# Output projection weights in two loads, powers of two one pass earlier, six mixer products ahead

## The chip, the cores and the metric

One core of one Trainium2 chip runs the kernel. The metric is the device time of one execution in microseconds (us); the figure for a kernel is the median of several runs. Engines are called by the names of the profile: PE multiplies matrices (PEld is its loading of the stationary operand), DVE and ACT work on vectors, POOL is hardly used here, SP issues most of the DMA transfers and ACT a few.

## The reference, cut to what matters

```
g = sigmoid((x * gate_w).sum(-1))                 # one gate per row
qkv = x @ wqkv                                    # 32 heads of 32
o = softmax(q . k at 8 positions, 2 apart) @ v    # sliding dilated window
a = o @ wo
z = gelu(x @ w_in); z1, z2 = z[:, :1792], layernorm(z[:, 1792:])
b = (z1 * (w_sp @ z2 + b_sp[:, None])) @ w_out    # mixer
out = g * a + (1 - g) * b                         # 2048 x 1024, bf16
```

## The kernel before, in words

All large buffers are regions of one tile in on-chip memory, `arena`, addressed by offsets. PSUM, the accumulation memory, is used as eight banks of 128x512; each product takes a bank and gives it back when the vector engines have read it.

PE works through these stages in order: the second half of z, the q/k/v projection (L478), the rest of z (L259, L515), the spatial mixing by w_sp in chunks of 512 output rows (`g_chunk`, L529), and then the output rows in sixteen blocks of 128, four blocks to a `final_chunk`. Rows 0 to 1023 of the mixing are plain products in `g_chunk(0)` and `g_chunk(1)`; rows 1024 to 2047 are done by `seven_products` (L645), seven half-size products in place of eight, between `final_chunk(1)` and `final_chunk(2)`. For these, the rows of w_sp are scaled by powers of two: `natural` loads 128 rows from ACT's queue (L570), `row_sums` (ACT) or `row_sums_fast` (DVE, L577) sums their absolute values, `row_powers` (DVE, L587 to L593) makes the powers, `scale_rows` multiplies on ACT (L611) and writes the rows to `wsp_d` from ACT's queue (L612), and `load_wsp` (L426) reads them back transposed on SP's queue.

The attention runs on DVE beside PE. For each of eight head groups `attention_steps` has a pass of q times k for two halves (L303 and the folds L306), the softmax, and a pass of probabilities times v for two halves (the product L336, the folds L342 and L343, the last one L339). The passes are software pipelined: group 7's q.k comes ahead of group 6's product with v, and group 7's product with v is last. q, k and v of a group are loaded to `q_t`, `k_t` and `v_t`, next to each other at `A_OFF`; the results of two groups are stored to `o_d` by `store_o` (L354).

One output block is, for each half of 512 columns, an attention product of 8 matmuls (`attn_mm`, L542, which needs the block of `o_d` transposed by `load_oT`, L397, in one of three slots, and `wo`), a mixer product of 14 matmuls (`mixer_mm`, L558), and `combine`: ACT scales the attention product (L565), DVE adds the mixer product (L566). Then SP stores the block (L739). `final_chunk(0)` makes the mixer products of blocks 0 and 1 (four of them, each holding a bank) ahead of everything else, and then calls `scaled_rows`.

wo lies at `A_OFF` as eight k tiles of 1024 columns, in the place of q, k and v and the beginning of the work buffer. `load_wo` makes four transfers (L394), one for each head of a group: head h goes to every fourth partition.

The order is written out by hand: a clock, `beat`, runs along with PE's columns; `beat.at(t, fn)` issues a piece of work when the clock passes t; DVE's steps carry their own lengths. That fixes each engine's order of instructions and each queue's order of transfers; only waits decide the times. Transfers signal eight counters in turn, and a transfer waits for the last one that had its counter. SP's queue at the end of the attention holds, in order: the load of v for group 7 (L350), the last `store_o`, the four of `load_wo`, `load_oT` for blocks 0, 1 and 2, `load_wsp(3, 0..3)`, the store of block 0, `load_oT(3)`, the store of block 1, `load_oT(4)`.

Of the kernel before, what the change touches and what calls it, by code (L numbers as in the profile page):

```python
# [17 lines left out]
D = 1024  # L18
KT = D // P
NH = 32  # L20
DH = 32
HG = 4
# [33 lines left out]
def kernel(  # L56
# [24 lines left out]
    def reg(off, n):  # L81
        return arena[:, off:off + n]
# [21 lines left out]
    for jh in range(2):  # L104
        for w in range(W):
            n = min(8, max(0, 14 - 2 * w - 8 * jh))
# [38 lines left out]
    wo_sb = reg(A_OFF, KT * D).rearrange("p (k n) -> p k n", k=KT)  # L145
# [38 lines left out]
    wo_v = A_wo.rearrange("(g h d) n -> g h d n", g=NG, h=HG, d=DH)  # L184
    sync = nc.sync
# [38 lines left out]
    beat = Beat()  # L224
# [74 lines left out]
    def qk_steps(jh):  # L299
        def mul():  # L300
            in0 = _sub_ap(q_t, (8 * jh) * C, [[0, W], [C, 8], [1, C]])
            in1 = _sub_ap(k_t, (8 * jh) * C, [[2 * C, W], [C, 8], [1, C]])
            TT(prod.rearrange("p (w j c) -> p w j c", w=W, j=8, c=C), in0, in1, ALU.mult)  # L303

        def fold(half):
            return lambda: TT(pv[:, :, 0:half], pv[:, :, 0:half], pv[:, :, half:2 * half], ALU.add)  # L306

        def last():
            TT(L[:, jh * 256:(jh + 1) * 256], pv[:, :, 0], pv[:, :, 1], ALU.add)

        return [(4.4, mul), (2.3, fold(16)), (1.2, fold(8)), (0.7, fold(4)), (0.6, fold(2)), (0.6, last)]
# [18 lines left out]
    def pv_steps(g, jh):  # L330
        o_out = obuf[:, :, (g % 2) * C:(g % 2 + 1) * C]

        def mul():
            in0 = _sub_ap(v_t, (8 * jh) * C, [[2 * C, W], [C, 8], [HG, DH], [1, HG]])
            in1 = _sub_ap(att_A, jh * 256, [[32, W], [HG, 8], [0, DH], [1, HG]])
            TT(prod.rearrange("p (w j d h) -> p w j d h", w=W, j=8, d=DH, h=HG), in0, in1, ALU.mult)  # L336

        def last():
            TT(o_out[:, 8 * jh:8 * jh + 8, :], p3[:, 0, :].rearrange("p (j c) -> p j c", c=C),  # L339
               p3[:, 1, :].rearrange("p (j c) -> p j c", c=C), ALU.add)  # L340

        return [(4.4, mul), (2.3, lambda: TT(p3[:, 0:4, :], p3[:, 0:4, :], p3[:, 4:8, :], ALU.add)),  # L342
                (1.2, lambda: TT(p3[:, 0:2, :], p3[:, 0:2, :], p3[:, 2:4, :], ALU.add)), (0.7, last)]  # L343

    def load_qk(g):
        sync.dma_start(q_t, bass.AP(tensor=q_d.tensor, offset=q_d.offset + g * S * C, ap=[[NJ * C, P], [1, NJ * C]]))
        sync.dma_start(k_t, bass.AP(tensor=k_d.tensor, offset=k_d.offset + (g * (S + 16) + 2) * C, ap=[[NJ * C, P], [1, NJJ * C]]))

    def load_v(g):
        sync.dma_start(v_t, bass.AP(tensor=v_d.tensor, offset=v_d.offset + (g * (S + 16) + 2) * C, ap=[[NJ * C, P], [1, NJJ * C]]))  # L350

    def store_o(g):
        dst = o_d[:, (g - 1) * C:(g + 1) * C].rearrange("(p j) c -> p j c", j=NJ)
        sync.dma_start(dst, obuf)  # L354

    def attention_steps(t):
        beat.at(t - 8.0, lambda: load_qk(0))
        beat.at(t - 7.9, lambda: load_v(0))
        for g in range(NG):
            for took, fn in qk_steps(0) + qk_steps(1):  # L360
                yield t, took, fn
            t = beat.vector
            if g + 1 < NG:
                beat.at(t + 1.0, lambda g=g: load_qk(g + 1))
            yield t, 2.4, soft_a
            t = beat.vector
            beat.at(t + (1.0 if g == 0 else 5.0), soft_exp)
            if g == 0:
                t += 5.0
            else:  # L370
                for took, fn in pv_steps(g - 1, 0) + pv_steps(g - 1, 1):
                    yield t, took, fn
                t = beat.vector
                if g + 1 < NG:
                    beat.at(t + 1.0, lambda g=g: load_v(g))
                else:
                    load_v(g)
                if g % 2 == 0:
                    beat.at(t + 1.5, lambda g=g: store_o(g - 1))
            yield t, 2.3, soft_b  # L380
            t = beat.vector
        for took, fn in pv_steps(NG - 1, 0) + pv_steps(NG - 1, 1):
            yield t + 5.0, took, fn
        t = beat.vector
        beat.at(t + 1.0, lambda: store_o(NG - 1))
        beat.at(t + 1.5, load_wo)
        for a in range(3):
            beat.at(t + 8.0, lambda a=a: load_oT(a))

    def load_wo():  # L390
        pitch = wo_sb.ap[0][0]
        for h in range(HG):
            dst = bass.AP(tensor=wo_sb.tensor, offset=wo_sb.offset + h * pitch, ap=[[pitch * HG, DH], [D, KT], [1, D]])
            sync.dma_start(dst, wo_v[:, h, :, :].rearrange("g d n -> d g n"))  # L394

    def load_oT(a):
        sync.dma_start_transpose(oT_slots[a % 3], o_d[a * P:(a + 1) * P, :])  # L397
# [141 lines left out]
    def attn_mm(a, n0, nw):  # L539
        psa = psum.tile([P, 512], F32, name="psa", tag="ps")  # L540
        for kt in range(KT):
            nc.tensor.matmul(psa[:, 0:nw], oT_slots[a % 3][:, kt, :], wo_sb[:, kt, n0:n0 + nw],  # L542
                             start=(kt == 0), stop=(kt == KT - 1))
        beat.run(KT * nw)
        return psa
# [9 lines left out]
    def mixer_mm(a, n0, nw):  # L555
        psb = psum.tile([P, 512], F32, name="psb", tag="ps")
        for f in range(NF):
            nc.tensor.matmul(psb[:, 0:nw], u_tile(f, a), w_out_sb[:, f, n0:n0 + nw],  # L558
                             start=(f == 0), stop=(f == NF - 1))
        beat.run(NF * nw)  # L560
        return psb
# [10 lines left out]
    def row_sums(r):  # L572
        for k in range(4):
            nc.scalar.activation(abs_out, nat_slots[r][:, 512 * k:512 * (k + 1)], ACT.Abs, accum_out=l1[:, r, k:k + 1])
# [9 lines left out]
    def row_powers(r0, r1, parts):  # L584
        v = nc.vector
        sl = slice(r0, r1)
        v.tensor_reduce(row[:, sl], l1[:, sl, 0:parts], AX.X, ALU.add)  # L587
        v.scalar_tensor_tensor(row[:, sl], b_in[:, sl], -1.0, row[:, sl], ALU.mult, ALU.max)
        TT(row[:, sl], row[:, sl], b_in[:, sl], ALU.max)
        v.tensor_scalar(row[:, sl], row[:, sl], TINY, None, ALU.max)  # L590
        v.tensor_scalar(expo[:, sl], row[:, sl].bitcast(I32), 23, None, ALU.logical_shift_right)
        v.tensor_scalar(up[:, sl], expo[:, sl], -1, 254 + TOP, ALU.mult, ALU.add)
        v.tensor_scalar(up[:, sl], up[:, sl], 23, None, ALU.logical_shift_left)  # L593
        beat.on_vector(0.9)
# [15 lines left out]
    def scale_rows(r):  # L610
        nc.scalar.activation(nat_slots[r], nat_slots[r], ACT.Copy, scale=up[:, r:r + 1].bitcast(F32))  # L611
        nc.scalar.dma_start(wsp_d[r], nat_slots[r])  # L612
# [101 lines left out]
    def final_chunk(c):  # L714
        first = {}
        if c == 0:
            for a in range(2):
                for n0 in (0, 512):
                    first[a, n0] = mixer_mm(a, n0, 512)
            beat.flush(1e9)  # L720
            scaled_rows()
        if c == 1:
            for k in range(5):
                beat.at(beat.now + 12.0 + 3.0 * k, lambda k=k: t_sums(k))
            for k in range(2):
                beat.at(beat.now + 28.0 + k, lambda k=k: s_sum(0, k))
        for a in range(4 * c, 4 * c + 4):
            ob = ob_slots[a % 3]
            if a > 0 and a + 2 < 16:
                load_oT(a + 2)  # L730
            last = a == 15
            for part, (n0, nw) in enumerate(((0, 512), (512, 384), (896, 128)) if last else ((0, 512), (512, 512))):
                psa = attn_mm(a, n0, nw)
                psb = first[a, n0] if (a, n0) in first else mixer_mm(a, n0, nw)
                combine(a, n0, nw, part % 2, psa, psb)
                if last:
                    sync.dma_start(out2[a * P:(a + 1) * P, n0:n0 + nw], ob[:, n0:n0 + nw])
            if not last:
                sync.dma_start(out2[a * P:(a + 1) * P, :], ob)  # L739
# [8 lines left out]
    t_rows = beat.now  # L748
    for k, r in enumerate((3, 4, 5, 6, 7)):
        natural(r)  # L750
        beat.at(t_rows + 6.0 + 3.5 * k, lambda r=r: row_sums(r))
        beat.at(t_rows + 32.0 + 3.0 * k, lambda r=r: scale_rows(r))
    beat.at(t_rows + 27.0, lambda: row_powers(3, 8, 4))
    beat.at(t_rows + 40.0, lambda: natural(0))
    g_chunk(1)
    final_chunk(0)
# [38 lines left out]
```

## Time and profile before

| | us |
|---|---|
| median of 3 runs | 710.26 (709.88 to 710.59) |
| the profiled execution | 711.12 |
| its span, first to last instruction | 709.3 |
| PE busy | 699.6 |
| DVE busy | 458.5 |
| ACT busy | 278.7 |

The span is 1.8 us shorter than the execution that it was taken from, and that execution is 0.9 us above the median. Start times in the profile are us from the start of the span; PE's granted clock is 0.998 on average over the span.

### The profile page before, as it was taken

To read this page: it belongs to the slowest core of one execution; us is meant where nothing else is said; L and a number is where in the kernel's file an instruction comes from. 1 tells how busy PE (TensorE), PEld (TensorE's weight loads), DVE (VectorE), ACT (ScalarE), POOL (GpSimd) and SP (SyncE) were. 2 spreads that over 40 slices of the span, in tenths; PEclk is the share of its full clock that TensorE was granted. 3 is DMA by queue.
4 is the path that set the end of the run, shared out by engine and by line. 5 is a ranking of instruction groups with operands and counts; after the bars stand their busy time and mean duration, and the time that the engine had idled before them with its cause. 6 is when DMAs were issued, how large, how long until landed. Compare 5 with 4: busy or idle time off the path is not lost. (4 is left out here: it accounts for less than half of the span.)

```text
span 709.3 us, 8465 instructions
## 1 busy us (share of the span) xinstructions
PE 699.6 (99%) x3319; PEld 359.6 (51%) x3319; DVE 458.5 (65%) x496; ACT 278.7 (39%) x508; POOL 14.0 (2%) x23
## 2 busy tenths in 40 slices
PE   8999999999999999999999999989999999999998
PEld 4466666666665554444444444434444444444444
DVE  0000498999999999999999999734153565731111
ACT  4434544435369886244341229435111222221111
POOL 1000000000000211000000000000000000000000
PEclk9999999999999999999999999999999999999999
DMA  9984974885573133885349940299942211202210
GB/s 227 192 178 97 259 192 113 216 192 157 145 203 121 56 101 60 210 287 175 107 142 276 357 169 36 76 351 261 179 112 67 69 33 57 45 0 60 60 44 31
DMA packets 182903, 101.29 MB, mean 143 GB/s; under 512 B 145744, under 2 KB 171344, under 8 KB 182608
## 3 DMA queue, kind: packets, MB, share of 16 engines
q1 hardware_dynamic: 180560, 92.37, 49.3%
q10 hardware_dynamic: 2304, 8.39, 3.2%
q8 instruction: 26, 0.43, 0.3%
q14 instruction: 13, 0.11, 0.0%
HBM read 51.91 MB, written 32.57 MB: 119 GB/s over the span
## 5 line engine op out<-in xcount | busy, mean ns | idle before, releaser
L478 PE MATMUL ps<-arena 128*128 128x512 bf16 x768 | 165.9, 379 | 0.0
L478 PEld LDWEIGHTS <-arena 128*128 128x128 bf16 x768 | 110.7, 144 | 55.1
L303 DVE TENSOR_TENSOR arena<-arena 128x8192 bf16<-128x8192 bf16 x16 | 70.8, 4423 | 53.2 <-DMA arena<-k_d 53.0
L558 PE MATMUL psb<-arena 128*128 128x512 bf16 (+2 forms) x462 | 101.6, 373 | 0.0
L259 PE MATMUL ps<-arena 128*128 128x512 bf16 (+1 forms) x512 | 97.7, 353 | 1.5 <-DMA arena<-in_B_w_in_dram 1.5
L529 PE MATMUL ps<-arena 128*128 128x512 bf16 x448 | 97.0, 379 | 0.0
L515 PE MATMUL ps<-arena 128*128 128x512 bf16 x448 | 96.9, 379 | 0.0
L481 ACT CAST arena<-ps 128x512 bf16<-128x512 f32 x96 | 55.8, 587 | 93.1 <-PE ps L478 88.6
L566 DVE SCALAR_TENSOR_TENSOR arena<-psb,omg,arena 128x512 bf16<-128x512 f32 (+2 forms) x33 | 24.2, 735 | 103.7 <-PE psb L558 88.3
L645 PE MATMUL ps<-arena 128*128 128x512 bf16 (+1 forms) x392 | 84.8, 379 | 0.0
L306 DVE TENSOR_TENSOR arena<-arena 128x4096 bf16<-128x4096 bf16 (+1 forms) x64 | 77.5, 1211 | 1.9
L259 PEld LDWEIGHTS <-arena 128*128 128x128 bf16 x512 | 50.0, 98 | 48.7 <-issue 2.0
L558 PEld LDWEIGHTS <-arena 128*128 128x128 bf16 x462 | 44.7, 98 | 52.1
L336 DVE TENSOR_TENSOR arena<-arena,att_A 128x8192 bf16<-128x8192 bf16 x16 | 70.7, 4421 | 0.2
L515 PEld LDWEIGHTS <-arena 128*128 128x128 bf16 x448 | 43.8, 98 | 52.7
L529 PEld LDWEIGHTS <-arena 128*128 128x128 bf16 x448 | 43.8, 98 | 52.6
L565 ACT ACTIVATE arena<-psa,g_s 128x512 f32<-128x512 f32 (+2 forms) x33 | 22.1, 674 | 120.8 <-PE psa L542 119.9
L542 PE MATMUL psa<-arena 128*128 128x512 bf16 (+2 forms) x264 | 61.5, 379 | 4.3 <-DMA arena<-in_A_wo_dram 4.3
L645 PEld LDWEIGHTS <-arena 128*128 128x128 bf16 (+1 forms) x392 | 38.3, 98 | 46.3
L517 ACT ACTIVATE arena<-ps 128x512 bf16<-128x512 f32 x56 | 31.7, 598 | 48.7 <-PE ps L515 37.1
L264 ACT ACTIVATE arena<-ps 128x512 bf16<-128x512 f32 (+1 forms) x64 | 34.3, 538 | 25.7 <-PE ps L259 25.6
L542 PEld LDWEIGHTS <-arena 128*128 128x128 bf16 x264 | 25.7, 99 | 35.7 <-DMA arena<-in_A_wo_dram 4.8
(93 smaller groups left out, 399.4 us busy)
## 6 DMA issues: line engine op xcount, KB each, us to landing
arena<-k_d SPq DMA_DIRECT2D x8, 960.0 KB, 6.9
arena<-v_d SPq DMA_DIRECT2D x8, 960.0 KB, 4.6
z_d<-arena SPq DMA_DIRECT2D x14, 512.0 KB, 3.4
arena<-in_A_wqkv_dram SPq DMA_DIRECT2D x24, 256.0 KB, 4.7
arena<-in_B_w_in_dram SPq DMA_DIRECT2D x4, 1024.0 KB, 6.7
q_d<-arena SPq DMA_DIRECT2D x32, 128.0 KB, 2.3
k_d<-arena SPq DMA_DIRECT2D x32, 128.0 KB, 2.3
v_d<-arena SPq DMA_DIRECT2D x32, 128.0 KB, 2.3
```

The lines of the kernel that those rows point to most:

```text
L259: nc.tensor.matmul(ps[:, 0:N], xT[:, kt, i * P:(i + 1) * P], w2[:, kt, ZC * c:ZC * c + N], start=(kt == 0), stop=(kt == KT - 1))
L264: nc.scalar.activation(z2[:, 4 * c:4 * c + n // P, i, :], ps[:, 0:n].rearrange("p (f q) -> p f q", q=P), ACT.Gelu_apprx_tanh, accum_out=s1 ...
L303: TT(prod.rearrange("p (w j c) -> p w j c", w=W, j=8, c=C), in0, in1, ALU.mult)
L306: return lambda: TT(pv[:, :, 0:half], pv[:, :, 0:half], pv[:, :, half:2 * half], ALU.add)
L336: TT(prod.rearrange("p (w j d h) -> p w j d h", w=W, j=8, d=DH, h=HG), in0, in1, ALU.mult)
L478: nc.tensor.matmul(ps[:].rearrange("p (t c) -> p t c", t=4), lhsT, wgt[:, :, kt, :], start=(kt == 0), stop=(kt == KT - 1))
L481: nc.scalar.copy(st[:, j % 4, :], ps[:])
L515: nc.tensor.matmul(ps[:], w1[:, kt, (f % 4) * P:(f % 4 + 1) * P], xT[:, kt, 512 * c:512 * (c + 1)], start=(kt == 0), stop=(kt == KT - 1))
L529: nc.tensor.matmul(ps[:], z2[:, f, i, :], wsp[:, i, :, :].rearrange("p a t -> p (a t)"), start=(i == 0), stop=(i == 15))
L542: nc.tensor.matmul(psa[:, 0:nw], oT_slots[a % 3][:, kt, :], wo_sb[:, kt, n0:n0 + nw], start=(kt == 0), stop=(kt == KT - 1))
L558: nc.tensor.matmul(psb[:, 0:nw], u_tile(f, a), w_out_sb[:, f, n0:n0 + nw], start=(f == 0), stop=(f == NF - 1))
L645: nc.tensor.matmul(dst[:], lhs[:, k, :], rhs(k), start=first and k == 0, stop=k == 7, skip_group_check=not first)
```

## The change

wo is loaded in two parts. Its k tiles 0 to 4 are issued after group 7's q.k pass, where for the earlier groups the next q and k would be loaded; they cover the place of `q_t` and most of `k_t`. Tiles 5 to 7, which cover the rest of `k_t`, `v_t` and the start of the work buffer, are loaded where all of wo was. Each part is four transfers, so there are eight instead of four. In the second place, `row_powers(3, 8, 4)` and the five `scale_rows` get earlier due times, and the `row_sums` are set a little closer. In the third, `final_chunk(0)` makes the mixer products of blocks 0, 1 and 2 ahead, six instead of four.

```diff
             if g + 1 < NG:
                 beat.at(t + 1.0, lambda g=g: load_qk(g + 1))
+            else:
+                beat.at(t + 1.0, lambda: load_wo(0, 5))
...
-        beat.at(t + 1.5, load_wo)
+        beat.at(t + 1.5, lambda: load_wo(5, KT))
...
-    def load_wo():
+    def load_wo(k0, k1):
         pitch = wo_sb.ap[0][0]
         for h in range(HG):
-            dst = bass.AP(tensor=wo_sb.tensor, offset=wo_sb.offset + h * pitch, ap=[[pitch * HG, DH], [D, KT], [1, D]])
-            sync.dma_start(dst, wo_v[:, h, :, :].rearrange("g d n -> d g n"))
+            dst = bass.AP(tensor=wo_sb.tensor, offset=wo_sb.offset + h * pitch + k0 * D,
+                          ap=[[pitch * HG, DH], [D, k1 - k0], [1, D]])
+            sync.dma_start(dst, wo_v[k0:k1, h, :, :].rearrange("g d n -> d g n"))
...
         if c == 0:
-            for a in range(2):
+            for a in range(3):
...
-        beat.at(t_rows + 6.0 + 3.5 * k, lambda r=r: row_sums(r))
-        beat.at(t_rows + 32.0 + 3.0 * k, lambda r=r: scale_rows(r))
-    beat.at(t_rows + 27.0, lambda: row_powers(3, 8, 4))
+        beat.at(t_rows + 6.0 + 3.3 * k, lambda r=r: row_sums(r))
+        beat.at(t_rows + 29.0 + 3.0 * k, lambda r=r: scale_rows(r))
+    beat.at(t_rows + 19.5, lambda: row_powers(3, 8, 4))
```

## The prediction

> **What bounds the kernel now.** First the page's busy times: PE 699.6 of 709.3 us, no other engine above 65%. What can be won without taking work from PE is where PE stands still. The list of waits, for PE alone, leaves one place worth a look:
>
> ```profile
> PE psa L542 <- DMA arena<-in_A_wo_dram: 4.3, 1, 4.3
> PE ps L259 <- DMA arena<-in_B_w_in_dram: 1.5, 2, 1.0
> ```
>
> The chain that ended last shows what that wait hangs on (start, length, what):
>
> ```profile
> 461.03 8.83 DMA wsp_d<-arena
> 469.88 9.00 DMA arena<-in_A_wo_dram
> 478.88 0.86 issue
> 479.74 10.25 PE psa L542 x40
> 489.99 3.02 PE psb L558 x14
> ```
>
> The fourth transfer of wo is held until a write of scaled rows to `wsp_d` has landed; they share nothing but a counter. It then needs 9 us, and PE starts its first attention product at 479.74. From there to the end the chain is PE without a break. Third, the timeline of that stretch, for SP's queue, the weight loads and ACT:
>
> ```profile
> 457.61 12.87 SPq L394 DMA_DIRECT2D arena<-in_A_wo_dram  x4
> ...
> 463.17 12.25 PE L558 MATMUL psb<-arena 128*128 128x512 bf16 x56
> ...
> 470.58 9.31 SPq L397 DMA_TRANSPOSE arena<-o_d  x3
> ...
> 480.00 12.25 SPq L426 DMA_TRANSPOSE arena<-wsp_d  x4
> ...
> 480.12 0.15 PEld L542 LDWEIGHTS <-arena 128*128 128x128 bf16 x1 [0.28 <-issue]
> ...
> 486.13 0.69 ACT L565 ACTIVATE arena<-psa,g_s 128x512 f32<-128x512 f32 x1 [0.44 <-ACT arena L611]
> ...
> 492.35 0.53 SPq L739 DMA_DIRECT2D out_dram<-arena  x1
> ...
> 492.99 2.09 SPq L397 DMA_TRANSPOSE arena<-o_d  x1
> ...
> 497.89 1.41 PEld L542 LDWEIGHTS <-arena 128*128 128x128 bf16 x8 [0.37 <-DMA arena<-o_d]
> ```
>
> Two things to see. After the wait the weight loads come 0.42 to 0.43 us apart for seven starts, twice a warm matmul's 3.02/14 = 0.216 us: PE restarts at half clock. And `load_oT(3)`, issued at 492.99, lands just as PE wants it at 497.89: a second transfer stands close behind wo. Last, the windows: transfers move 371 GB/s from 463 to 475.4, but 0 GB/s from 411 to 416.
>
> **The change part by part.** Removed: the four mixer products should have ended at 463.17 + 56 x 0.216 = 475.25, so the wait cost 4.49 us; the 40 attention matmuls from 479.74 to 489.82 took 10.08 us against 8.63 warm, so the half clock cost 1.45. With the little at 497.89 about 6.1 us can be had (497.89 less the 491.8 worked out below), no more.
>
> *Six products ahead.* The same matmuls in another order, cost nothing on PE. They end at 463.17 + 84 x 0.216 = 481.3. Even the old wo (479.7) would be there by then, so this part alone removes the wait for wo. But the six attention products now follow one another, then the small transpose of the biases (0.15), so PE wants `load_oT(3)` at 481.3 + 48 x 0.216 + 0.15 = 491.8 instead of 497.9. Six banks are held and two are left. In the built program the third attention product takes the bank that ACT's first L565 frees, the fourth that of DVE's first L566, and so on. With the spacing of before (L565 0.69, then L611 1.99, next L565 3.0 later) the first L565 ends at 483.7, the first L566 at 484.5, the second pair at 486.7 and 487.5; PE asks at 484.8, 486.5, 488.2 and 490.0. Each is free 1.1 us or more ahead: 0. The cover is gone if DVE's chain for rows 0 to 2 (483.5 before) ends past 485; its loads come earlier (below).
>
> *Early tiles.* In the built order they stand behind `store_o` and wait for DVE's product L336 of group 6, first half, which ran 407.01 to 411.43. SP then issues four, each 0.60 to 1.84 us, into an idle DMA. DVE's next L336, at 418.73 before, waits for all four, since their region counts as overlapping with the work buffer. Last issue 411.4 + 3 x 0.96 = 414.3; landing 4.6 (the 960 KB load of v, median) gives 418.9, a delay d of 0.2. Bounds: d = 0, or 416.9 + 11.0 (wo's slowest landing, on full queues) = 427.9, 9.2 us. I take 0.2, because the DMA is empty there. Behind SP's four stands the load of v, which before went at 423.17; ACT's last `natural` waits for the first of the four, landing near 416, before it went at about 419. What DVE loses, the last `store_o`, all of SP's queue behind it and ACT's drains lose too. PE has about two drained tiles' lag and eight banks, so it does not feel d directly.
>
> *Late tiles.* 0.77 MB where 2.1 MB stood. In the new turn of counters the fourth waits for `store_o` (landed by 462 before) and not for a `wsp_d` row. That takes 6.9 us of waiting out of SP's queue.
>
> *Powers ahead.* DVE's seven small steps move from 452.25 to behind the L343 that ended at 443.35, and ACT's sums ended near 440.8, so DVE waits for nothing (if ACT is up to 2 us late, still nothing). They take 1.4 us there and give it back before the last L339: 0. ACT's first L611 goes from 453.66 to about 447, the last `wsp_d` write from 467.6 to about 461.5, the last two `natural` from 468.3 to about 464. No PE term; it unloads the queue.
>
> *What is late next: SP's queue ahead of* `load_oT(3)`. `load_oT(0)` waits for the first late transfer: 457.61 + 9.5 = 467.1 (470.58 before). Then three `load_oT` and four `load_wsp`: 21.8 us as before would bring SP to the store of block 0 at 488.9; at their uncongested lengths (1.3 and 2.5 each) at 481. The store itself waits for DVE's second L566, 487.5. I take 487.5, as about 1 MB less is in flight (2.7 us at 371 GB/s off the 21.8), then 0.64 to the transfer: issue 488.2. Landing 4.4, the median of the sixteen: 492.6. PE wanted it at 491.8 and waits 0.8. Bounds: landing 3.1 (the shortest) gives 491.3, no wait; 488.9 with 5.6 (the median of this stretch) gives 495.1, 3.3 us.
>
> **Sum.** The point that both kernels share is the start of block 3's attention product: 497.89 before, 492.6 after, 5.3 us earlier, and what follows on PE is the same work. The later `load_oT` are 9.5 us of PE apart (two times 1.73 + 3.02), and their SP entries have two stores and a few transposes in between, as before. The profiled execution, 711.12, would become 705.8; the median stands 0.86 below it, so I say 705.0.
>
> A page bears on the half clock. The Trainium skill (TensorE: Matmul & The Clock Gate, Part 1: The HAM clock gate) says that an idle window of about 3.4 us halves PE's clock and that it needs about 3.4 us of work to come back. The trace agrees on the kind: 4.49 us idle, seven starts at half speed. As an estimate by that page the restart costs 1.7 us, and the sum would give 704.8. What no run shown here can say yet is whether a wait of 1 to 3 us stays free of it.
>
> **The rivals.**
>
> *The gain is cut by a late* `load_oT(3)`. For it: SP's queue is in strict order, seven transposes lie ahead, and before they kept SP busy without a break from 470.58 to 492.25. Against it: the queue starts 3.5 us earlier. If SP passes them at 489.5 and the landing takes 5.6, PE starts block 3 at 495.7, 2.2 us gained: 708.1.
>
> *The wait only moves.* If the queue is no faster than before, `load_oT(3)` lands at 497.9 and PE idles 6 us ahead of block 3 instead of ahead of block 0, half clock included or not: about 710.3. For it: the six products alone would do just this. Against it: 6.9 us of waiting leaves the queue.
>
> *Slower.* The early tiles hold DVE at L336. The last `store_o`, and behind it all of SP's queue, is late by the same d, and it is `load_oT(3)` that ends last. It decides from the point where SP issues the store of block 0 later than 490.9: then block 3's operand lands past 490.9 + 0.64 + 4.9 = 496.4, PE idles 4.6 us, longer than the wait that cost it the half clock, and pays 1.45 again. From 487.5 to 488.9 that needs a d of 2 to 6 us or more. With d at its bound of 9.2 SP reaches the store at 481 to 488.9 plus 9.2, say 494; block 3 starts at 499.5 and half clock makes that 501, 3.1 us behind: 713.4. For it: the L336 wait is real, and five `natural` of 512 KB enter the same queues at 416. The Trainium skill (Trainium Kernel Development and Optimization, Key Constraints) says the transfers of SP's and ACT's queues share the same 16 engines and interleave; as rows here the `natural` landed in 5.5 to 7.9 us at 377 GB/s. Against it: the four are issued 2 to 5 us ahead of them into 0 GB/s.
>
> **How the numbers follow.** Forecast 0.68; cut 0.14; moved 0.08; slower 0.10. The forecast's own range is 704.2 (all of 6.1) to 706.2 (landing 5.6 at 488.2: 4.1). A measurement here can tell 0.2%, 1.4 us, from no change, so faster means under 708.84. The forecast and most of the cut case lie there: 0.81; same 0.08; slower 0.11. For 8 in 10 the range takes the forecast, widened by the spread of the runs (0.4) at the low end, and the cut case with 0.3 beyond its 708.1 + 0.4: 703.8 to 708.8.
>
> **What would show it.** L394 as two groups, the first issued near 411 to 414, with L336 of group 6's second half starting near 419. Row powers near 443.4. No PE wait for wo; `psb` as one run of 84 from 463 to 481, `psa` following at 0.216. The last of SP's four `load_wsp(3)` ending before 488.5, the store of block 0 waiting for DVE and not for the queue, and at most 1 us of PE waiting for `o_d` ahead of block 3, without half clock. Wrong if L336 waits over 3 us, if ACT or DVE hold a bank (PE waiting for L565 or L566 between 484 and 492), or if the `o_d` wait exceeds 3 us.

## The result, and the profile after

The changed kernel takes 705.96 us (median of 7 runs, 705.06 to 706.58), the kernel before beside it 710.59 (7 runs): a ratio of 0.9921, with a 95% interval of 0.9894 to 0.9949. The prediction was 705.0, in a range of 703.8 to 708.8: the time lies in it, 0.96 above the point. Of that, 0.33 is the kernel before, whose median rose from 710.26 to 710.59 with more runs; the other 0.63 is a smaller gain, 4.63 us by the medians where 5.26 was forecast, and is found below.

The profiled execution took 706.58 us, span 704.8, 4.54 less than that of before (711.12). In the code after, lines from L394 on stand three lower: L397 is now wo's load, L400 `load_oT`, L429 `load_wsp`, L545 the attention product, L561 the mixer product, L569 DVE's part of `combine`, L573 `natural`, L580 `row_sums_fast`, L590 to L596 `row_powers`, L614 and L615 the scaling and its write, L742 the store.

The list of waits of the changed kernel, PE alone (us in total, times, longest). The wait for wo is gone; `load_oT(3)` is now the only one after 460 us:

```profile
PE psa L545 <- DMA arena<-o_d: 1.3, 1, 1.3
PE pw L97 <- PEq L782: 0.8, 1, 0.8
PE ps L259 <- DMA arena<-in_B_w_in_dram: 0.6, 2, 0.5
```

The chain that ended last, around that wait (start, length, what). It runs through PE alone until it meets one transfer of 5.09 us:

```profile
483.42 4.72 PE psa L545 x22
488.14 5.09 DMA arena<-o_d
493.23 0.05 issue
493.28 1.90 PE psa L545 x8
```

The timeline of the changed kernel, lines of SP, DVE, ACT and PE (start, length, engine, line, operation, idle time before in brackets):

```profile
410.33 2.65 SPq L397 DMA_DIRECT2D arena<-in_A_wo_dram  x4
...
417.61 4.42 DVE L336 TENSOR_TENSOR arena<-arena,att_A 128x8192 bf16<-128x8192 bf16 x1
...
442.14 0.17 DVE L590 TENSOR_REDUCE row<-l 128x5 f32<-128x20 f32 x1
...
446.55 2.00 ACT L614 ACTIVATE arena<-arena,up 128x2048 bf16<-128x2048 bf16 x1
...
456.27 6.56 SPq L397 DMA_DIRECT2D arena<-in_A_wo_dram  x4
...
463.13 18.29 PE L561 MATMUL psb<-arena 128*128 128x512 bf16 x83
...
473.52 11.00 SPq L429 DMA_TRANSPOSE arena<-wsp_d  x4
...
481.26 10.52 PE L545 MATMUL psa<-arena 128*128 128x512 bf16 x47
...
487.69 0.35 SPq L742 DMA_DIRECT2D out_dram<-arena  x1
488.14 1.31 SPq L400 DMA_TRANSPOSE arena<-o_d  x1
...
493.28 1.90 PE L545 MATMUL psa<-arena 128*128 128x512 bf16 x8 [1.34 <-DMA arena<-o_d]
```

Read it from top to bottom as the path of the change. wo's first part enters an idle queue at 410.33; DVE's next L336 starts 11.72 us after the one before it, as before (407.01 to 418.73). The row powers run at 442.14 and the first scaling at 446.55. wo's second part takes SP 6.56 us, where all of wo took 12.87. The whole of DVE runs 1.1 us earlier than in the profile of before, and did so ahead of the change's first transfer (the L336 before that one started at 405.89, against 407.01). PE then runs 84 mixer matmuls (83 recorded) and 48 attention matmuls (47) without a wait and at full clock: the seven weight loads at 0.42 us have no counterpart. At the end stands a wait of 1.34 us, and the eight matmuls behind it take 1.90 us, the warm time.

A measure that is free of what lies ahead is the distance from the first mixer product of `final_chunk(0)` to block 3's attention product, since both orders do the same matmuls in between. Before it was 497.89 - 463.17 = 34.72 us, after 493.28 - 463.13 = 30.15: 4.57 us, which is the whole gain of the profiled execution.

### The profile page after: what moved, and what is told of

Read it like the earlier page. It is cut to its first block, busy times and chain, and to the rows that moved or that the text cites. A ratio compares the mean times of both kernels' runs of the same rounds, so it can differ in the third digit from the quotient of the medians.

```text
span 704.8 us, 8427 instructions
## 1 busy us (share of the span) xinstructions
PE 696.2 (99%) x3270; PEld 359.6 (51%) x3319; DVE 458.3 (65%) x496; ACT 279.1 (40%) x508; POOL 14.0 (2%) x23
## 4 chain that ended last, share of the span: by engine, by line
PE 97%; DMA 1%; issue 0%; SPq 0%; DVE 0%; DVEq 0%
PE ps L481 24%; PE ps L532 14%; PE psb L561 14%; PE ps L518 14%; PE ps L259 13%; PE ps L648 12%; PE psa L545 7%; DMA arena<-in_B_w_in_dram 1%; DMA arena<-o_d 1%; SPq L439 0%; SPq L437 0%; SPq L441 0%; DVE arena L569 0%; PE pt L584 0%; DVEq L569 0%
## 5 line engine op out<-in xcount | busy, mean ns | idle before, releaser
L561 PE MATMUL psb<-arena 128*128 128x512 bf16 (+2 forms) x453 | 100.7, 372 | 0.5
L259 PE MATMUL ps<-arena 128*128 128x512 bf16 (+1 forms) x501 | 97.6, 353 | 1.3 <-DMA arena<-in_B_w_in_dram 0.6
L569 DVE SCALAR_TENSOR_TENSOR arena<-psb,omg,arena 128x512 bf16<-128x512 f32 (+2 forms) x33 | 24.1, 734 | 104.9 <-PE psb L561 80.2
L648 PE MATMUL ps<-arena 128*128 128x512 f16 (+1 forms) x385 | 84.4, 379 | 0.4
L561 PEld LDWEIGHTS <-arena 128*128 128x128 bf16 x462 | 44.6, 98 | 52.1
L336 DVE TENSOR_TENSOR arena<-arena,att_A 128x8192 bf16<-128x8192 bf16 x16 | 70.7, 4421 | 0.2
L545 PE MATMUL psa<-arena 128*128 128x512 bf16 (+2 forms) x260 | 59.5, 372 | 1.6 <-DMA arena<-o_d 1.3
L545 PEld LDWEIGHTS <-arena 128*128 128x128 bf16 x264 | 25.5, 98 | 31.2 <-DMA arena<-o_d 1.5
```

The lines of the kernel that those rows point to most:

```text
L259: nc.tensor.matmul(ps[:, 0:N], xT[:, kt, i * P:(i + 1) * P], w2[:, kt, ZC * c:ZC * c + N], start=(kt == 0), stop=(kt == KT - 1))
L648: nc.tensor.matmul(dst[:], lhs[:, k, :], rhs(k), start=first and k == 0, stop=k == 7, skip_group_check=not first)
```

## The experiments

The three edits were tried alone and in pairs, and then two further edits. In the table "tiles" is the split of wo, "powers" the earlier powers of two, "six" the six mixer products, "own place" an edit of our own: block 3's operand gets a place that no other block uses. "Block 3" is the distance just defined, in one profiled execution; with a +, PE afterwards ran at half clock for some us, which comes on top of the distance (in the kernel before it lies within).

| kernel | tiles | powers | six | own place | PE's wait for `o_d` | block 3 | median us (range, runs) | ratio to before |
|---|---|---|---|---|---|---|---|---|
| before | | | | | 0 (4.32 for wo) | 34.72 | 710.59 (709.73 to 716.06, 7) | |
| six_only | | | x | | 7.86 | 37.09 + | 713.35 (707.20 to 714.30, 12) | 1.0028 [1.0011, 1.0046] |
| tiles_only | x | | | | 5.64 | 34.55 + | 711.99 (708.84 to 716.48, 12) | 1.0020 [1.0001, 1.0039] |
| tiles_six | x | | x | | 2.61 | 31.93 + | 711.26 (706.61 to 712.80, 12) | 1.0008 [0.9993, 1.0023] |
| powers_only | | x | | | 1.57 | 30.68 | 708.38 (706.13 to 712.97, 8) | 0.9982 [0.9957, 1.0006] |
| powers_six | | x | x | | 1.18 | 29.98 | 706.38 (704.94 to 711.83, 12) | 0.9965 [0.9945, 0.9985] |
| tiles_powers | x | x | | | 1.08 | 30.00 | 704.62 (704.54 to 705.93, 5) | 0.9936 [0.9923, 0.9949] |
| after_again (the change) | x | x | x | | 1.33 | 30.14 | 705.71 (705.08 to 705.96, 5) | 0.9944 [0.9932, 0.9957] |
| powers_spare | | x | | x | 0 | 29.23 | 705.10 (704.66 to 706.11, 6) | 0.9905 [0.9875, 0.9936] |
| oT_spare | x | x | x | x | 0 | 28.74 | 704.62 (704.44 to 704.85, 5) | 0.9931 [0.9917, 0.9944] |

Each ratio is to the kernel before on the same chip, whose median was 710.29, 709.71 and 711.27 in the three sets of runs; powers_spare is from the third set, so its ratio isn't to be held against that of oT_spare, but their distances can be.

### Six products alone

```diff
         if c == 0:
-            for a in range(2):
+            for a in range(3):
```

> Only the six mixer products ahead; wo in one piece, powers as before. Theory (two gates: wo ahead of block 0, then load_oT(3) ahead of block 3, and the later one decides): wo lands near 479.7, under the sixth product that ends at 481.3, so PE no longer waits for wo. SP's queue is as before, the store of block 0 goes near 492.3 and load_oT(3) lands near 497.9, while PE wants it at 491.8. PE idles about 6 us there; if that costs the half clock again, 1.45 on top: block 3 starts at 497.5 to 498, the whole at 710 to 712, not faster. Rival (the wait for wo was the only gate): block 3 starts at 491.8, the whole near 704.5.

This is the rival "the wait only moves" by itself. The timeline of six_only:

```profile
481.01 11.57 SPq L426 DMA_TRANSPOSE arena<-wsp_d  x4
...
493.31 2.10 SPq L397 DMA_TRANSPOSE arena<-o_d  x1
...
499.20 3.60 PE L542 MATMUL psa<-arena 128*128 128x512 bf16 x8 [7.86 <-DMA arena<-o_d]
```

PE no longer waits for wo, but SP's queue is as before and `load_oT(3)` is issued at 493.31, so PE waits 7.86 us ahead of block 3. The eight matmuls behind it take 3.60 us instead of 1.90. The wait moved and grew, and the kernel is 0.28% slower. The two gates of the theory are there; the time is 1.35 us above its range, as the wait was 7.86 and not 6, and the half clock cost 2.22 us (499.20 to 506.17 for 22 matmuls that take 4.75 warm).

### Early tiles alone

The hunks of the change on `load_wo`, nothing else.

> Only the early tiles of wo; four products ahead, powers as before. Theory: what matters is SP's queue. The late part of wo lands before 475, PE goes on at 475.25 without a wait, the queue reaches the store of block 0 at 487 to 488 and load_oT(3) lands at 492.5 to 493.5; block 3 starts there, the whole at 705 to 706.5, as with all three parts. Rival (six products are needed as a cover, or the powers, which come as late as before, hold ACT and with it the banks): PE waits at 475 or between 482 and 490, block 3 starts at 495 or later, the whole at 708 or more.

Here the theory fell; the time is the rival's, but PE waits for `load_oT(3)` and not where the rival put the wait. The timeline of tiles_only shows that the part does what the prediction credits it with, and that it is worth nothing:

```profile
455.11 6.78 SPq L397 DMA_DIRECT2D arena<-in_A_wo_dram  x4
...
469.59 15.55 SPq L429 DMA_TRANSPOSE arena<-wsp_d  x4
...
485.87 2.18 SPq L400 DMA_TRANSPOSE arena<-o_d  x1
...
496.64 3.60 PE L545 MATMUL psa<-arena 128*128 128x512 bf16 x8 [5.64 <-DMA arena<-o_d]
```

SP spends 6.78 us on wo instead of 12.87, and PE has wo in time. `load_oT(3)` is even issued 23.78 us after the first mixer product, 1.2 us earlier than in the changed kernel (25.01), but lands only just before 496.64, some 10.7 us after its issue. The four transposed loads of w_sp keep SP for 15.55 us (11.00 in the changed kernel). Windows of 5 us of tiles_only (length, busy us of PE, PEld, DVE, ACT, POOL with counts, granted clock, DMA share, GB/s; the share adds up the times of packets in flight and can pass 1):

```profile
475.00:480.00 5.00, 5.00 (x24) 2.25 (x23) 3.92 (x7) 0.69 (x1) 0.00 (x0) 1.00 1.33 160
...
485.00:490.00 5.00, 5.00 (x25) 2.15 (x24) 1.41 (x2) 4.11 (x6) 0.00 (x0) 1.00 1.23 123
```

and the same two windows of the changed kernel:

```profile
475.00:480.00 5.00, 5.00 (x25) 2.28 (x24) 2.47 (x12) 0.00 (x0) 0.00 (x0) 1.00 0.91 179
...
485.00:490.00 5.00, 5.00 (x25) 2.29 (x24) 0.77 (x2) 4.09 (x5) 0.00 (x0) 1.00 0.69 218
```

In tiles_only the DMA engines are full from 485 to 490 (share 1.23) and yet move 123 GB/s; in the changed kernel they have room (0.69) and move 218. So an early issue alone doesn't help `load_oT(3)`: what counts is how fast the transfers around it get through.

### Powers ahead alone

The last six changed lines of the diff, nothing else: wo is loaded in one piece, and four mixer products come ahead of it.

> Only the powers of two one pass ahead; wo in one piece, four products ahead. The write of scaled rows that held the fourth transfer of wo until 469.9 is issued near 455.5 and lands near 461. Theory (the hold by the counter, not the amount of data, made wo late): wo's fourth goes near 463 and lands by 473 to 475; PE waits at most 1 us at 475.25; SP reaches the store of block 0 at 488 to 490, block 3 starts at 493 to 495, the whole at 706 to 708. Rival (2.1 MB of wo in the busy stretch are too many, whatever the holds): PE still waits 3 us or more for wo, the whole at 709 to 710.5.

The timeline of powers_only:

```profile
454.98 8.04 SPq L394 DMA_DIRECT2D arena<-in_A_wo_dram  x4
...
487.51 1.97 SPq L397 DMA_TRANSPOSE arena<-o_d  x1
...
492.90 1.90 PE L542 MATMUL psa<-arena 128*128 128x512 bf16 x8 [1.57 <-DMA arena<-o_d]
```

The wait for wo disappears although wo's load is as it was: SP's four transfers take 8.04 us instead of 12.87. It is the counter: SP's list of waits had, before,

```profile
SPq L394 <- DMA wsp_d<-arena: 6.9, 1, 6.9
```

and in powers_only the four wait for `store_o` alone, 3.3 us, since the `wsp_d` row is written earlier. `load_oT(3)` lands in 5.3 us. ACT's last two `natural` are issued at 462.49, against 467.54 in tiles_only, and land at 470.32 and 472.35, before the four transposed loads of w_sp begin (474.84). The distance of block 3 is 0.53 us longer than with the whole change.

But this holds in half of the runs: 706.13, 706.85, 707.29 and 707.55 at a mean granted clock of 1.000, and 709.21, 709.67, 712.69 and 712.97 at 0.995 to 0.998. The profile is of one of the first four. A lower mean clock is what the half clock behind a wait leaves (0.992 to 0.997 in the profiles that have one, 0.998 in that of before), so the others probably have a longer wait; none of them was profiled. Over all runs the interval of the ratio includes 1: alone, the powers are not shown to make the kernel faster.

### Early tiles and six products, without the powers

> Early tiles and six products, powers as before: all but the second part of the change. Theory: the powers for rows 0 to 2 end near 483.3 on DVE as before, 1 us before they hold a bank, and SP's queue is unloaded by the tiles: block 3 starts at 492.5 to 494, the whole at 705 to 706.8, within 0.8 us of the full change. Rival (the powers are what lets the queue through): SP reaches the store of block 0 past 490, PE waits 3 us or more for load_oT(3), the whole at 708 or more.

The change without the powers is no faster than the kernel before (ratio 1.0008). The timeline of tiles_six, which is of one of its quicker runs (709.39):

```profile
472.34 15.53 SPq L429 DMA_TRANSPOSE arena<-wsp_d  x4
...
488.78 0.35 SPq L742 DMA_DIRECT2D out_dram<-arena  x1
489.22 1.30 SPq L400 DMA_TRANSPOSE arena<-o_d  x1
...
494.40 2.55 PE L545 MATMUL psa<-arena 128*128 128x512 bf16 x8 [2.61 <-DMA arena<-o_d]
```

The same 15.5 us for four transposed loads as in tiles_only, and 153 GB/s from 475 to 480. PE waits 0.19 us for a bank at 486.13 and 2.61 us ahead of block 3, then runs the next 22 matmuls in 6.44 us instead of 4.75. But the way is another than in tiles_only. Here `load_oT(3)` lands 5.13 us after its issue, as in the changed kernel (5.09); it is issued 26.75 us after the first mixer product instead of 25.01. SP had been free since 487.87, and the store of block 0 ahead of it waited for DVE, whose sum of the last row began only at 481.14, when that `natural` landed (its powers ended at 484.8, against 477.3 in the changed kernel). So late rows cost time in two ways, over DVE and in the DMA engines, and the powers are the part without which the rest gains nothing.

### The change again, and with one part left out

> The changed kernel once more, as the measure for the others on this chip: 0.990 to 0.995 of the kernel before, block 3 starting 30 us after the first mixer product (30.15 in its first profile; 34.72 before), PE waiting 1 to 2 us for load_oT(3) without half clock.

> Powers ahead and six products, wo in one piece: the full change without the early tiles. Theory (the last two loads of unscaled rows and the writes to wsp_d have to be out of the way before SP's four transposed loads of scaled rows; the powers do that, and the tiles only help): block 3 starts 30.5 to 32 us after the first mixer product, with a wait of 1.5 to 3 us for load_oT(3), in some executions with half clock on top; 706 to 709, within 2.5 us of the full change. Rival (the tiles carry the gain): 34 us or more, 710 or more.

> Early tiles and powers ahead, four products ahead: the full change without the six. Theory: the late part of wo lands before the fourth product ends, load_oT(3) is the only gate left and PE wants it at the same time with four products ahead as with six; block 3 starts 29.5 to 31 us after the first mixer product, 704.5 to 707, as the full change. Rival (the six give wo or load_oT(0) time that they need): PE waits at the first attention product, the whole 1 us or more above the full change.

The change repeats in another set of runs: 705.71, ratio 0.9944, a wait of 1.33 us. Without the tiles (powers_six) the quickest runs are as quick, 704.94, but they reach to 711.83; the five above 708 us have a granted clock of 0.995 to 0.998, the seven below 0.999 to 1.000. With the tiles, no run is above 706.6 us in after, after_again or tiles_powers, and none has a granted clock under 0.999. So what the early tiles bring to powers and six products is the absence of slow runs; by the medians the two don't differ clearly (0.9965 and 0.9944, with intervals that overlap). Without the six products they bring more: 0.9936 for tiles_powers against 0.9982 for powers_only, and those intervals are apart.

Without the six products (tiles_powers) nothing is lost: 704.62 against 705.71, with intervals that overlap. The chain of tiles_powers shows why they add nothing:

```profile
485.25 7.34 DMA arena<-o_d
492.59 0.05 issue
492.64 1.90 PE psa L545 x8
```

With four products ahead, block 0 is finished earlier, so `load_oT(3)` is issued 22.61 us after the first mixer product, 2.4 us ahead of the changed kernel (25.01). It takes 7.34 us instead of 5.09 and lands 29.95 us after the first mixer product, against 30.10 in the changed kernel and 30.09 in after_again. The earlier issue met fuller DMA engines (a share of 1.19 from 485 to 490, against 0.69) and gained 0.15 us.

### A place of its own for block 3's operand

```diff
+    oT_spare = reg(A_OFF + 20480, 1024).rearrange("p (k t) -> p k t", k=KT)
...
-        for a in range(3):
+        for a in range(4):
             beat.at(t + 8.0, lambda a=a: load_oT(a))
...
+    def oT_at(a):
+        return oT_spare if a == 3 else oT_slots[a % 3]
...
-            if a > 0 and a + 2 < 16:
+            if a > 1 and a + 2 < 16:
                 load_oT(a + 2)
```

> The full change, and the operand of block 3 has a place of its own (where a sum for the seven products is kept later), so that it is loaded with blocks 0 to 2 and waits for no product and no store. Theory (load_oT(3) is the last gate in the changed kernel): PE has no wait between the first mixer product and block 4; block 3 starts 28.6 to 28.8 us after the first mixer product; 1.3 to 2 us under the full change and a smaller spread, 703.8 to 705. Rival (the next transfer in SP's order is as late): PE waits 1 us or more for block 4 or later, no gain over the full change.

`load_oT(3)` no longer waits for block 0's slot and goes with the first three. The waits of oT_spare, PE alone, and its timeline:

```profile
PE ps L260 <- DMA arena<-in_B_w_in_dram: 1.1, 2, 0.7
PE pw L97 <- PEq L786: 0.8, 1, 0.8
```

```profile
465.25 9.65 SPq L404 DMA_TRANSPOSE arena<-o_d  x4
...
491.30 1.90 PE L549 MATMUL psa<-arena 128*128 128x512 bf16 x8
```

PE has no wait left in this stretch. The distance is 28.74 us, 1.40 less than in after_again, and the time 704.62 us (704.44 to 704.85) against 705.71 (705.08 to 705.96) on the same chip: no run of the one reaches the other. So the 1.33 us were all that `load_oT(3)` still cost. By the medians it is 1.09 us, less than the 1.3 that were expected at least, and tiles_powers has the same median (704.62) with one run at 705.93.

### Are the transposed loads of w_sp the backlog?

In tiles_only, the four `load_wsp(3)` went behind `load_oT(4)`:

```diff
-            load_wsp(3, r)
+            beat.at(t + 19.0 + 3.0 * r, lambda r=r: load_wsp(3, r))
```

> Early tiles alone (four products ahead, powers as late as before), and the four load_wsp(3, ...), which stood ahead of the store of block 0 in SP's queue, are issued after load_oT(4) instead. In tiles_only these four took SP 15.6 us and load_oT(3) behind them landed 10.6 us after its issue. Theory (with the powers late, the transposed loads run into the last loads of unscaled rows and the writes to wsp_d, and load_oT(3) waits in the queues behind them): without them load_oT(3) lands within 3 to 6 us of its issue and before 490, block 3 starts 28.6 to 30 us after the first mixer product, the whole near 704.5 to 706. Rival (the loads and writes of the rows themselves make load_oT(3) late): it lands 8 us or more after its issue, block 3 at 33 us or more, 709 or more.

If those four loads as such were at fault, the kernel would be near 705. It is worse: 714.25 us (708.50 to 717.77, 12 runs), ratio 1.0032 [1.0005, 1.0059]. The timeline of tiles_wsp_late, and one of its windows:

```profile
463.96 13.13 SPq L400 DMA_TRANSPOSE arena<-o_d  x3
...
486.34 6.76 PE L545 MATMUL psa<-arena 128*128 128x512 bf16 x23 [6.74 <-DMA arena<-o_d]
486.37 2.29 DVE L580 TENSOR_REDUCE l<-arena 128x1 f32<-128x2048 bf16 x1 [0.43 <-DMA arena<-in_B_w_sp_dram]
...
494.02 0.35 SPq L742 DMA_DIRECT2D out_dram<-arena  x1
494.47 1.30 SPq L400 DMA_TRANSPOSE arena<-o_d  x1
```

```profile
470.00:475.00 5.00, 4.95 (x23) 2.04 (x21) 2.11 (x1) 0.00 (x0) 0.00 (x0) 1.00 1.46 79
```

Now the three small transposes of `o_d` take SP 13.13 us (7.40 to 10.63 in the other kernels that load three there), with a full DMA (1.46) that moves 79 GB/s, and PE waits 6.74 us for one of them. The last two `natural` were issued at 467.54 and 469.82, and DVE has the last row only at 486.37. For `load_oT(3)` neither theory nor rival holds in full: it lands 4.9 us after its issue, as the theory said, but it is issued only at 494.47, since the store of block 0 waits for DVE. Block 3 starts 38.19 us after the first mixer product.

So the slow stretch is there whichever transposes stand in it. In tiles_only, tiles_six and tiles_wsp_late the last row landed at 476.8, 481.1 and 486.3, in the midst of the transposes. In the changed kernel DVE begins on the last row at 473.6, as the four loads of w_sp begin (473.52). In the kernel before the rows were as late as in tiles_only (478.75), but the four began at 480.00, behind wo, and took 12.25 us. That plain and transposed transfers hinder one another is an inference from this pattern; why the rate falls wasn't settled.

### Powers and the own place, without tiles and six products

> Powers ahead and the place of its own for block 3's operand, but wo in one piece and four products ahead. Theory (powers ahead make wo land in time, since the counter that held its fourth transfer comes free; the place of its own removes the gate at block 3; tiles and six products add nothing more): no PE wait over 0.5 us, 704.3 to 705.5, as with all parts. Rival (without tiles wo or load_oT(0) is late in part of the executions): a median of 706 or more, or a spread of 3 us or more, as in powers_only.

705.10 us, no run above 706.11, with a distance of 29.23. PE waits for neither wo nor `o_d`; a gap of 0.33 us that no semaphore explains stands ahead of the first attention product. The expectation held. So two small edits, earlier powers and one more slot, do what the three parts do, and the gain doesn't need the split of wo.

### How long may PE wait before it slows down?

The prediction left open whether a wait of 1 to 3 us stays free of the half clock. In the kernel of oT_spare, PE was made to wait four times, behind blocks 8, 10, 12 and 14, for copies of chosen lengths on ACT. They add work and take none away:

```diff
+    waits = {8: (512,), 10: (1152,), 12: (1792,), 14: (1280, 1280)}
+
+    def hold(psb, widths):
+        nc.scalar.copy(gl_s[:, 0:8], psb[:, 0:8])
+        for n in widths:
+            nc.scalar.copy(reg(CD_OFF, n), reg(CD_OFF + 4096, n))
+        pt = psum.tile([P, P], BF, name="pt", tag="ps")
+        nc.tensor.transpose(pt[:], reg(CD_OFF, P), ident[:])
...
+                if part == 1 and a in waits:
+                    hold(psb, waits[a])
```

idle_b has the widths 2048, 1536, 1024 and 1408 in their place.

> oT_spare with four waits for PE put in behind blocks 8, 10, 12 and 14: ACT copies a strip of 512, 1152, 1792 and 2 x 1280 columns (unused data) and PE waits for it. Waits of about 1.3, 1.9, 2.5 and 3.8 us are expected. Theory (what the runs so far show: 1.6 us free, 2.6 us not): the matmuls behind the first two keep 0.216 us, behind the last two they start at 0.43. Rival (only a wait over 3.4 us does it, and in tiles_six something else slowed PE): only behind the last. About 9.5 us longer in waits, 1.5 more for each half-clock stretch.

> As idle_a with 2048, 1536, 1024 and 1408 columns, which gives waits of about 2.7, 2.3, 1.8 and 2.1 us. Theory: half clock behind the first, full clock behind the third; the bound lies between 1.6 and 2.6 us, so the other two tell where. Rival (only over 3.4 us): full clock behind all four.

One execution of each: 719.63 and 720.76 us. The timeline of idle_a at its second and third wait, and of idle_b at its second and third:

```profile
656.46 0.23 PE L728 MATMUL pt<-ident,arena 128*128 128x128 bf16 x1 [2.16 <-ACT arena L726]
656.52 1.89 PE L549 MATMUL psa<-arena 128*128 128x512 bf16 x7
...
678.38 0.23 PE L728 MATMUL pt<-ident,arena 128*128 128x128 bf16 x1 [2.70 <-ACT arena L726]
678.45 2.55 PE L549 MATMUL psa<-arena 128*128 128x512 bf16 x8
```

```profile
660.99 0.23 PE L728 MATMUL pt<-ident,arena 128*128 128x128 bf16 x1 [2.49 <-ACT arena L726]
661.06 1.89 PE L549 MATMUL psa<-arena 128*128 128x512 bf16 x7
...
682.27 0.23 PE L728 MATMUL pt<-ident,arena 128*128 128x128 bf16 x1 [2.06 <-ACT arena L726]
682.34 2.66 PE L549 MATMUL psa<-arena 128*128 128x512 bf16 x8
```

Eight attention matmuls in 1.89 us are warm, 2.55 or 2.66 are partly at half clock. Waits of 1.71, 2.16, 2.38 and 2.49 us left the clock alone; 2.06, 2.70, 2.98 and 3.56 halved it, at a cost of 1.68 us, once 2.94 (after 2.98). So the theory of idle_b fell on its third wait, which was to stay at full clock. 2.06 did and 2.49 didn't, so the length of the wait doesn't decide alone. With the other profiles: waits of 1.08 to 1.57 us were free in all five kernels that had one, 2.61 us and more never.

The granted clock in these traces says what decides. In idle_b it changes between full and half at 635.52, 642.35, 683.31 and 686.72, that is 2, 12 and 1 steps of 3.41 us apart; wherever a profile has several changes, they lie on such a grid. Cut the time into these steps and add up how long PE stood still in each:

| run | wait | step, start to end | PE stood still | clock in the next step |
|---|---|---|---|---|
| idle_b | 2.49 | 656.00 to 659.42 | 0.91 | full |
| idle_b | 2.49 | 659.42 to 662.83 | 1.58 | full |
| idle_b | 2.06 | 679.90 to 683.31 | 2.06 | half |
| idle_b | 2.38 | 703.79 to 707.20 | 1.77 | full |
| idle_a | 1.71 | 631.74 to 635.15 | 1.70 | full |
| idle_a | 2.16 | 652.22 to 655.63 | 1.34 | full |
| idle_a | 2.70 | 676.11 to 679.53 | 2.27 | half |
| tiles_six | 2.61 | 492.09 to 495.50 | 2.31 | half |
| six_only | 7.86 | 490.05 to 493.47 | 2.13 | half |

The wait of 2.49 us is divided by the border at 659.42; the shorter one of 2.06 lies in one step. In all the profiles, no step at full clock with up to 1.77 us of standing still was followed by half clock, and each of the nine with 2.06 us or more was. The time after the last matmul of a kernel fits as well: a step with 1.89 us of it kept the clock (after_again), one with 2.01 lost it (powers_six). The half clock begins at the border and not with the work: after the wait of 2.06 us PE ran at full clock from 682.27 to 683.31. The wait of 2.98 us cost more since its last 0.80 us lay in the first step at half clock, and a second one followed.

## Why the prediction was right, and where it wasn't

| step of the prediction | said | measured |
|---|---|---|
| delay of DVE's L336 by the early tiles | 0.2 (0 to 9.2) | 0 |
| row powers on DVE | behind the L343 that ended at 443.35 | 442.14 to 443.5, behind that L343, with all of DVE 1.1 us earlier |
| first scaling, last `wsp_d` write | 447, 461.5 | 446.6, 461.6 |
| last two `natural` | 464 | 463.4 |
| six products end on PE | 481.3 | 481.3 |
| PE waits for a bank | 0 | 0 |
| store of block 0, set by DVE's second L566 | 487.5 | 487.7 |
| issue of `load_oT(3)` | 488.2 | 488.14 |
| its landing | 4.4 | 5.09 |
| PE's wait for it | 0.8 | 1.34, clock not halved |
| start of block 3 | 492.6 (5.3 earlier) | 493.28 (4.6 earlier) |

*The mechanism was right.* The wait for wo, 4.49 us, and the 1.45 of the half clock went, and `load_oT(3)` is the next gate, at the time that its store and DVE set. The mis-sized term is the landing, 4.4 taken as a median of all, 5.09 measured: 0.69 us, about what the gain fell short by. The median of that very stretch before, 5.6, stood in the text as a bound and was nearer.

*The weighing of the parts was wrong,* though the sum came out. The step on the powers said "No PE term; it unloads the queue", and the step on the late tiles gave those the credit: "That takes 6.9 us of waiting out of SP's queue". The runs show another weight. Tiles_only takes the 6.9 us out and gains nothing, since the transposes behind them crawl; powers_only removes the wait for wo with wo's load as it was, and in its profiled execution, one of the quicker half, `load_oT(3)` lands 1.57 us after PE wants it. The prediction had the facts for this: the fourth transfer of wo was held by a `wsp_d` row, so an earlier row frees it. That the sum came out was in part luck: the powers were in the change without a price of their own, and the same reasoning without them, the expectation of tiles_six, said 705 to 706.8 where 711.26 was measured.

*The rival "the wait only moves"* was given 0.08, with "6.9 us of waiting leaves the queue" against it. That reason was no evidence: in tiles_only the waiting left the queue and the wait moved all the same. What kept this rival from the changed kernel is the powers, as tiles_six shows. For the six products alone it is the exact description, "the six products alone would do just this", and with the half clock it is slower than before.

*The rival "cut by a late* `load_oT(3)`*"* was right in its place and too large: 0.7 us of gain cut, not 3.

*The rival "slower"* needed DVE to be held at L336 by 2 to 6 us. It was held by nothing: the early tiles had an idle DMA, and the load of v was issued 4.44 us after the start of that product, as before.

*The half clock.* The prediction drew on the Trainium skill (TensorE: Matmul & The Clock Gate, Part 1: The HAM clock gate) with an idle window of about 3.4 us and some 3.4 us to recover. The Trainium skill calls this window free-running in the same section: it doesn't reset when a kernel starts. The runs agree with the length, steps of 3.41 us with half clock for one to three of them, and with borders that fall inside waits and inside work. They disagree on how much idling it takes: 2.06 us within one step halved the clock. As an estimate by that page, a restart costs half of 3.4, 1.7 us; the runs agree in most cases (1.41 to 1.82 us; 2.22 in six_only, 2.94 once in idle_b). This couldn't have moved the sum to 704.8, as the prediction says: the sum goes by the arrival of `load_oT(3)` at 492.6, and the price of the old half clock doesn't enter it. Its open question has this answer: waits of 1.08 to 1.71 us were free, 2.06 to 2.49 were free or not by where the border fell, 2.61 and more never were.

## What to carry to other kernels

When a wait is removed, price the next one behind it as a second gate, and ask of it what is in the DMA engines with it, not only when its queue issues it: here the same transfer issued 2.4 us earlier landed 0.15 us earlier. A transfer that waits for a counter can be cured by bringing forward the unrelated transfer that had the counter last. Here that cheap edit was the one that nothing else replaced; alone it gave most of the gain in half of the runs, and with either the early tiles or a place of its own for block 3's operand in all of them. And test the parts of a change singly and in pairs: a sum that comes out right doesn't show that its terms were.

## What the runs showed of the hardware

- PE's granted clock changes on a grid of 3.41 us that doesn't start with the wait. A step with 2.06 us or more of standing still was followed by half clock (nine of nine), one with up to 1.89 us never. So a wait of 2.06 us cost 3.74 in all (1.68 for the half clock), and one of 2.49 us, divided by a border, nothing more than itself. The half clock cost 1.4 to 2.9 us each time.
- With transposed loads and plain loads and writes of 512 KB in flight together, the DMA engines moved as little as 79 GB/s at a share of 1.46 (tiles_wsp_late, 470 to 475). Before, they moved 417 GB/s at a share of 1.03 (470 to 475, wo and rows in flight). So a full DMA share doesn't tell the rate.
- The runs of one kernel can part into groups: powers_six has seven of 704.94 to 706.83 us at a granted clock of 0.999 to 1.000 and five of 708.22 to 711.83 at 0.995 to 0.998. One profile of such a kernel shows one of them; what the slower five waited for wasn't profiled.
